# A new written order for a fused attention and expert kernel, with 46 operations on other engines

## The chip, the core and the metric

The kernel runs on one core of a Trainium2 chip. The core has five engines that work side by side, each through its own list of instructions and strictly in that list's order: PE (TensorE, matrix products; its weight loads are shown as PEld), DVE (VectorE), ACT (ScalarE), POOL (GpSimd) and SP (SyncE, which here issues the DMAs). Operands lie in SBUF, products in PSUM. The metric is the device time of one execution in microseconds; less is better.

## What is computed

```python
# q, k, v: 8 batches x 8 heads x 576 tokens x 64; w_gate, w_val: 512 x 1536; w_out: 1536 x 512
k_p = k.reshape(B, H, 72, 8, D).mean(axis=3)
v_p = v.reshape(B, H, 72, 8, D).mean(axis=3)
scores = np.matmul(q, k_p.transpose(0, 1, 3, 2)) / 8
scores = scores - scores.max(axis=-1, keepdims=True)
attn = np.exp(scores)
attn = attn / (attn.sum(axis=-1, keepdims=True) + 1e-09)
x = heads_side_by_side(np.matmul(attn, v_p))     # 4608 tokens x 512
g = x @ w_gate
out = (g / (1 + np.exp(-g)) * (x @ w_val)) @ w_out
```

## The kernel before

**Stages.** The 4608 tokens go through in 9 tiles of 512. The attention of each batch gives its rows of `x` in pieces of at most 128 tokens, 40 in all; one piece is an "answer" (numbers 0 to 39; tile 3 is made of answers 13 to 17). An answer is: scores on PE (L983), maximum and sums on DVE, exponentials on ACT, the shares split into a high half (a 16-bit copy, ACT) and a low half (what the copy lost, L1053 and L1063 with a small second part, on DVE or POOL), a transposing DMA, and the product with the pooled values on PE. Answers 5 to 39 are divided by the softmax sums behind that product, by one DVE operation (L1092) or by eight on ACT, one a head (L1100), and are turned by another DMA into `x` of the expert. Answers 0 to 4 are divided ahead of it (L1034), and their result goes straight into the first tile's `x`: a high half on ACT (L1103) and a low half on DVE (L1107). That tile's products of gate and value read both halves (L1192, L1193, L1194).

**Decoding the weights.** Gate and value weights come as 64-bit numbers in 12 chunks of 128 columns. For each chunk `w_shift` (L732, DVE) moves the low word into place, `w_sign` makes a sign (POOL, DVE or ACT by chunk), `w_abs` (L751, ACT) makes the magnitude of the high word times 2^-112 as a 32-bit float, and `w_join` (L755, DVE) shifts that by three bits and puts the low word's bits in. `w_sums` (L766, ACT) and a PE product (L701) find a scale, and each of a chunk's two halves is then split into 16 bits (`w_high`, L784, ACT or POOL) and the rest (`w_low`, L789, DVE). Chunk by chunk the steps of the first tiles begin as their halves come ready.

**Steps.** Tiles 0 and 1 use `plain_step`. Tiles 2 to 8 use `fast_step`: seven products of six matmuls (L1295) in place of eight, which need sums of the weights (`fast_weights`, once) and of each tile's `x` (`fast_x`). `fast_x` runs twice a tile: one sum on DVE, four differences (L1260), a 16-bit copy on ACT (L1261), two differences for what the copy lost (L1264); L1260 and L1264 go to POOL for the tiles in `SUMS_ON_POOL`, otherwise to DVE. Inside a step the second and third product are joined by a DVE addition (L1360), the seventh and fourth by an ACT copy and a DVE addition (L1365), and the first product waits for an ACT copy (L1355). Behind each step ACT and DVE make the activation (L1139, L1142, L1147). Beside tile 8 the weights of the last product are summed (L1878 ACT, L1884 DVE and others), and then the output stages follow, from about 640 us on.

**The order.** The program is written as many small jobs (an answer, a chunk, a step, ...), and three long tables say whose turn it is at each operation (`NAMES`, `TURNS`) and which job gets which buffer (`HOLDERS`). Each engine's list is thus fixed ahead of time. Tuples of numbers beside them say which engine does certain operations: `DIVIDED_ON_ACT` (answers with L1100), `ON_POOL` (answers among 0 to 4 whose division, L1034, is POOL's), `LOW_ON_DVE` (answers whose low half is DVE's, else POOL's), `XT_ON_DVE` (the low half of the turned result, DVE or POOL), `WEIGHTS_ON_DVE` and `CUT_W_ON_DVE` (parts of `fast_weights` and of the last product's weights), `SUMS_ON_POOL` (tiles whose `fast_x` is POOL's).

Of the kernel before, what the change touches and what calls it, by code (L numbers as in the profile page):

```python
# [2352 lines left out]
```

## Time and profile before

| | |
|---|---|
| time, median of 3 runs | 900.15 us (899.26 to 900.62) |
| profiled execution | 900.0 us, span 898.2 us |
| busy: PE, DVE, ACT, POOL | 876.0, 732.5, 613.5, 193.7 us |
| PE idle, by the waits that the profile names | about 16 us |
| first product of the first tile's steps | 43.0 us |

The profiled execution gives busy time by engine and by stretch, the waits of each engine with what ended them, and every instruction in order of time. A stretch in which PE is busy all the time is bound by PE, and another engine's work there costs nothing until PE has to wait for it.

### The profile page before, as it was taken

Reading aid. Unit: us, or ns where it says so; the run is one execution under the profiler, and the core shown is the slowest. Engines: PE = TensorE matmul, PEld = TensorE weight load, DVE = VectorE, ACT = ScalarE, POOL = GpSimd, SP = SyncE. Lnnn points to the kernel's source line nnn. Section 1 sums busy time; section 2 is a strip of 40 time slices with the busy share of each in tenths; the row PEclk is TensorE's granted clock in tenths of the full one; section 3 lists DMA queues with packets and bytes.
Section 4 is the critical chain, followed back from the end, with each engine's and each line's share of the span. In section 5 each row is a group of like instructions: output and inputs, shape, how many; then the busy total and the mean of one; then the engine's idle time right before and its main releaser. Section 6 shows DMA issues by size and latency. Waiting matters only on the chain. (4 is left out here: it accounts for less than half of the span.)

```text
span 898.2 us, 18137 instructions
## 1 busy us (share of the span) xinstructions
PE 876.0 (98%) x6872; PEld 637.5 (71%) x6872; DVE 732.5 (82%) x1175; ACT 613.5 (68%) x1458; POOL 193.7 (22%) x245
## 2 busy tenths in 40 slices
PE   8899999999999999999999999999999999999998
PEld 5475455447888888888888888888885555555554
DVE  6998998899898788788888777577889686785963
ACT  5999845657768665865666765446558678696783
POOL 2565216558811421110101000023100000000000
PEclk9699999999999999999999999999999999999999
DMA  8968786547467596485475542436264530806212
GB/s 322 325 198 230 204 235 188 116 133 206 112 200 177 118 232 167 140 212 160 133 190 139 145 142 79 154 107 221 95 217 162 186 119 9 343 13 269 83 47 82
DMA packets 139127, 148.39 MB, mean 165 GB/s; under 512 B 85792, under 2 KB 107040, under 8 KB 136736
## 3 DMA queue, kind: packets, MB, share of 16 engines
q1 hardware_dynamic: 139040, 147.24, 54.7%
q8 instruction: 54, 0.88, 0.4%
q14 instruction: 33, 0.27, 0.1%
HBM read 87.29 MB, written 40.89 MB: 143 GB/s over the span
## 5 line engine op out<-in xcount | busy, mean ns | idle before, releaser
L1295 PEld LDWEIGHTS <-mixed 128*128 128x128 f16 x1494 | 144.5, 98 | 20.3 <-issue 2.4
L2148 PE MATMUL ps<-low,wsh 128*128 128x512 bf16 (+1 forms) x420 | 146.7, 358 | 0.0
L1295 PEld LDWEIGHTS <-wgv_h 128*128 128x128 f16 x1328 | 127.8, 98 | 21.0 <-issue 4.4
L1295 PE MATMUL ps<-xc,mixed 128*128 128x256 f16 x996 | 130.7, 273 | 0.6 <-ACT ps L1357 0.6
L1295 PE MATMUL ps<-xc,wgv_h 128*128 128x256 f16 x664 | 116.6, 273 | 1.6 <-DVE ps L1365 1.0
L1295 PE MATMUL ps<-x,wgv_h 128*128 128x256 f16 x664 | 116.7, 273 | 1.3 <-ACT rs L1355 1.3
L1139 ACT ACTIVATE hf<-ps,un 128x512 f32<-128x512 f32 (+1 forms) x111 | 75.5, 681 | 30.3 <-PE ps L1295 17.7
L1295 PE MATMUL ps<-x,wgv_l 128*128 128x256 f16 x332 | 90.5, 273 | 0.0
L1295 PE MATMUL ps<-xc,wgv_l 128*128 128x256 f16 x332 | 90.5, 272 | 0.0
L1147 DVE SCALAR_TENSOR_TENSOR hf<-ps,un,hf 128x512 f32<-128x512 f32 (+1 forms) x111 | 80.7, 729 | 10.7 <-PE ps L1295 8.1
L1193 PE MATMUL ps<-x,wgv_h 128*128 128x512 f16 (+1 forms) x224 | 80.5, 359 | 2.0 <-DVE x L1107 2.0
L1192 PE MATMUL ps<-x,wgv_h 128*128 128x512 f16 (+1 forms) x224 | 80.6, 360 | 0.9 <-ACT x L1103 0.8
L1194 PE MATMUL ps<-x,wgv_l 128*128 128x512 f16 (+1 forms) x224 | 80.5, 359 | 0.0
L1142 DVE SCALAR_TENSOR_TENSOR hf<-hf,ps 128x512 f32<-128x512 f32 (+1 forms) x111 | 73.3, 662 | 8.2 <-ACT hf L1139 8.1
L2148 PEld LDWEIGHTS <-wsh 128*128 128x128 bf16 x420 | 41.0, 98 | 45.2 <-issue 7.6
L2149 PE MATMUL ps<-top,wsl 128*128 128x512 bf16 x192 | 72.8, 379 | 0.0
L1295 PEld LDWEIGHTS <-wgv_l 128*128 128x128 f16 x664 | 64.9, 98 | 7.6
L1295 PE MATMUL ps<-x,mixed 128*128 128x256 f16 x498 | 68.0, 273 | 1.1 <-DVE ps L1360 1.1
L1002 ACT ACTIVATE sc<-ps,mx 128x72 f32<-128x72 f32 (+1 forms) x208 | 63.9, 331 | 0.7
L1357 ACT COPY ps<-ps 128x256 f32<-128x256 f32 x83 | 30.5, 368 | 46.8 <-PE ps L1295 46.3
L1365 DVE TENSOR_TENSOR ps<-ps,rs 128x256 f32<-128x256 f32 x83 | 35.3, 427 | 32.9 <-ACT ps L1364 32.7
L1355 ACT COPY rs<-ps 128x256 f32<-128x256 f32 x83 | 31.0, 373 | 33.2 <-PE ps L1295 22.8
(215 smaller groups left out, 1940.6 us busy)
## 6 DMA issues: line engine op xcount, KB each, us to landing
hd<-hf SPq DMA_DIRECT2D x105, 256.0 KB, 2.7
in<-kv_parts SPq DMA_DIRECT2D x42, 576.0 KB, 5.7
ws<-w_all SPq DMA_DIRECT2D x36, 512.0 KB, 5.4
wgv_h<-hd SPq DMA_DIRECT2D x9, 1536.0 KB, 7.7
wgv_l<-hd SPq DMA_DIRECT2D x9, 1536.0 KB, 7.6
out_t<-ob SPq DMA_DIRECT2D x36, 256.0 KB, 2.3
qt<-q_rows SPq DMA_DIRECT2D x32, 256.0 KB, 4.0
wd<-wf SPq DMA_DIRECT2D x12, 256.0 KB, 2.3
```

The costliest lines, as they stand in the source:

```text
L1002: nc.scalar.activation(sc[:n, h], pss[g][:n, j * SP : (j + 1) * SP], AF.Exp, bias=mx[:n, g, j : j + 1], scale=EXPSCALE, accum_out=sm[:n, h ...
L1139: nc.scalar.activation(hf, gate, AF.Tanh, scale=un[:, c, 0:1])
L1142: nc.vector.scalar_tensor_tensor(out=hf, in0=hf, scalar=1.0, in1=gate, op0=ALU.add, op1=ALU.mult)
L1147: nc.vector.scalar_tensor_tensor(out=out, in0=val, scalar=un[:, c, 2:3], in1=hf, op0=ALU.mult, op1=ALU.mult)
L1192: nc.tensor.matmul(o, wh, x["h"][:, j, a:e], start=(j == 0), stop=False)
L1193: nc.tensor.matmul(o, wh, x["l"][:, j, a:e], start=False, stop=False)
L1194: nc.tensor.matmul(o, wl, x["h"][:, j, a:e], start=False, stop=(j == NJ - 1))
L1295: nc.tensor.matmul(o, a, b, start=begin and j + n == 0, stop=j == HJ - 1 and n == 2, skip_group_check=True,)
L1355: tr = yield op("ACT", 380, lambda: nc.scalar.copy(rs, r), t5, tr)
L1365: tp = yield op("DVE", 430, lambda: nc.vector.tensor_add(s, s, rs), tp)
L2148: nc.tensor.matmul(o, top, where[1][:, c], start=False, stop=False, skip_group_check=True)
L2149: nc.tensor.matmul(o, lo, x_up, start=False, stop=c == HC - 1, skip_group_check=True)
```

## The change

Operations get other engines. `w_abs` of chunks 0, 1, 6 and 11 goes from ACT to DVE, as a product by 2^-112 that leaves the sign in place (the shift by three in `w_join` moves it out). One half's `w_high` goes from ACT to DVE, and the two that were POOL's go to ACT. Nothing is in the new tuples `SOFT_ON_DVE` and `X_ON_DVE`, so those two new paths don't run. The other tuples change as shown. The three tables are written anew throughout; a line or two stand for them.

```diff
-HIGH_ON_POOL = (11, 21)
+HIGH_ON_POOL = ()
+HIGH_ON_DVE = (1,)
+ABS_ON_DVE = (0, 1, 6, 11)
+SOFT_ON_DVE = ()
+X_ON_DVE = ()
...
-DIVIDED_ON_ACT = (14, 16, 18, 21, 22, 38)
+DIVIDED_ON_ACT = (6, 7, 8, 16, 19, 25, 30)
...
-ON_POOL = (1, 2, 3, 4, 5, 6, 7, 8, 9)
-LOW_ON_DVE = (1, 7, 9, 14, 15, 16, 19, 21, 23, 24, 26, 28, 29, 32, 34, 35, 37, 38, 39)
-XT_ON_DVE = (1, 2, 6, 7, 11, 12, 13, 16, 20, 21, 22, 27, 29, 30, 32, 33, 38, 39)
-WEIGHTS_ON_DVE = (1, 2, 4, 11)
-CUT_W_ON_DVE = (3, 4, 7)
-SUMS_ON_POOL = (4,)
+ON_POOL = (0, 1, 2, 3, 4, 5, 6, 7, 8, 9)
+LOW_ON_DVE = (0, 23, 33)
+XT_ON_DVE = (1, 2, 5, 11, 12, 13, 20, 21, 27, 28, 31, 34, 36, 37)
+WEIGHTS_ON_DVE = (1, 2, 4, 6, 9)
+CUT_W_ON_DVE = (2, 3, 4, 7)
+SUMS_ON_POOL = (3, 4, 5, 6, 7, 8)
...
 NAMES = (
-    "keys.0.0 keys.0.1 ask.0 values_load.0.0 warm chunk.0 values_load.0.1 chunk.1 first_fields answer.0 values_in.0.0 ask.1 values_load.0.2 "
+    "warm keys.0.0 keys.0.1 ask.0 values_load.0.1 chunk.0 values_load.0.0 first_fields answer.0 ask.1 values_in.0.1 chunk.1 chunk.2 "
...
     def w_abs(c):
+        if c in ABS_ON_DVE:
+            nc.vector.tensor_single_scalar(chunks[c]["wf"], chunks[c]["high"].bitcast(F32), 2.0**-112, ALU.mult)
+            return
         nc.scalar.activation(chunks[c]["wf"], chunks[c]["high"].bitcast(F32), AF.Abs, scale=2.0**-112)
...
         sw = chunks[c]["sw"]
+        if eng is nc.vector:
+            eng.tensor_scalar(hi, part(c, i), sw[:, i : i + 1], None, op0=ALU.mult)
+            return
...
+        elif 2 * c + i in HIGH_ON_DVE:
+            t = yield op("DVE+", 410, lambda: w_high(c, i, nc.vector), t)
```

The order on the engines is shown at two places. `mixed<-ws` is a chunk's magnitude, `wgv_h` and `wgv_l` the halves of its weights, `x` the first tile's input, `sc` scores, `half` the split shares; line numbers of the kernel after are larger by up to 23.

First ACT at the start of the program, behind the maximum of answer 0's scores. Before:

```order
L751 ACTIVATE mixed<-ws 128x1024
L1002 ACTIVATE sc,sm<-ps,mx 128x72 x8
L766 ACTIVATE wgv_h,wm<-mixed,least 128x512 x2
L1029 ACTIVATE sm<-sm,tiny 128x8
L746 ACTIVATE ws<-ws 128x1024
L751 ACTIVATE mixed<-ws 128x1024
L1017 ACTIVATE sc<-sc 128x576
L784 ACTIVATE wgv_h<-mixed,sw 128x512 x2
L1029 ACTIVATE sm<-sm,tiny 128x8
L1047 CAST half_142<-sc 128x512
L1049 CAST half_142<-sc 128x2x32 x2
```

After:

```order
L1012 ACTIVATE sc,sm<-ps,mx 128x72 x8
L1039 ACTIVATE sm<-sm,tiny 128x8
L773 ACTIVATE wgv_h,wm<-mixed,least 128x512 x2
L1062 CAST half_142<-sc 128x512
L1064 CAST half_142<-sc 128x2x32 x2
L1027 ACTIVATE sc<-sc 128x576
L750 ACTIVATE ws<-ws 128x1024
L1039 ACTIVATE sm<-sm,tiny 128x8
L794 ACTIVATE wgv_h<-mixed,sw 128x512
L750 ACTIVATE ws<-ws 128x1024
L758 ACTIVATE mixed<-ws 128x1024
```

Two magnitudes that stood here on ACT are gone from it (of chunks 0 and 1), the exponentials of answer 0 come right behind the score's maximum, and a chunk's first high half is alone here.

DVE ahead of the low half of the first piece's second `x` (L1107, after L1125). Before:

```order
L1020 TENSOR_REDUCE sm<-sc 128x8
L1107 SCALAR_TENSOR_TENSOR x<-ps,rr,x 128x4x128
L732 TENSOR_SCALAR ws<-ws 128x1024
L706 TENSOR_SCALAR p2w<-ps 128x2
L709 RECIPROCAL sw<-p2w 128x2
L1625 TENSOR_REDUCE spare<-in 128x144
L1024 RECIPROCAL ri<-sm 128x8
L789 SCALAR_TENSOR_TENSOR wgv_l<-mixed,sw,wgv_h 128x512 x2
L1107 SCALAR_TENSOR_TENSOR x<-ps,rr,x 128x4x128
```

After:

```order
L1030 TENSOR_REDUCE sm<-sc 128x8
L710 TENSOR_SCALAR p2w<-ps 128x2
L713 RECIPROCAL sw<-p2w 128x2
L1646 TENSOR_REDUCE spare<-in 128x144
L1034 RECIPROCAL ri<-sm 128x8
L736 TENSOR_SCALAR ws<-ws 128x1024
L710 TENSOR_SCALAR p2w<-ps 128x2
L713 RECIPROCAL sw<-p2w 128x2
L1125 SCALAR_TENSOR_TENSOR x<-ps,rr,x 128x4x128
L799 SCALAR_TENSOR_TENSOR wgv_l<-mixed,sw,wgv_h 128x512
L762 SCALAR_TENSOR_TENSOR mixed<-mixed,ws 128x1024
L799 SCALAR_TENSOR_TENSOR wgv_l<-mixed,sw,wgv_h 128x512
```

Before, two low halves of weights (L789) stand directly ahead of that `x`; after, `x` (the L1125 row) stands ahead of the two (L799), with a chunk's `w_join` (L762) between them.

Second, the sums of tile 3's `x`. Before, they stand in DVE's list, among the additions of tile 2's steps:

```order
L1260 TENSOR_TENSOR fx<-fx 128x256
L1142 SCALAR_TENSOR_TENSOR hf<-hf,ps 128x512
L1360 TENSOR_TENSOR ps<-ps,rs 128x256
L1625 TENSOR_REDUCE box<-in 128x144 x2
L1142 SCALAR_TENSOR_TENSOR hf<-hf,ps 128x512
L1147 SCALAR_TENSOR_TENSOR hf<-ps,un,hf 128x512
L1360 TENSOR_TENSOR ps<-ps,rs 128x256
L1264 TENSOR_TENSOR xc<-fx,xc 128x512
L1024 RECIPROCAL ri<-sm 128x8
L1365 TENSOR_TENSOR ps<-ps,rs 128x256
L1264 TENSOR_TENSOR xc<-fx,xc 128x512
```

After, they stand in POOL's list, among low halves of answers (L1078, L1079) and parts of `fast_weights` (L1240):

```order
L1282 TENSOR_TENSOR xc<-fx,xc 128x512
L1254 TENSOR_TENSOR wgv_l<-room,wgv_h 128x256
L1078 TENSOR_TENSOR half_142<-sc,half_142 128x8x56
L1079 TENSOR_TENSOR half_142<-sc,half_142 128x128
L1282 TENSOR_TENSOR xc<-fx,xc 128x512
L1078 TENSOR_TENSOR half_143<-sc,half_143 128x8x56
L1079 TENSOR_TENSOR half_143<-sc,half_143 128x128
L1278 TENSOR_TENSOR fx<-fx 128x256 x4
L1240 TENSOR_TENSOR fw<-fw 128x256
L1282 TENSOR_TENSOR xc<-fx,xc 128x512 x2
L1840 TENSOR_TENSOR box<-sc,box 128x512
```

The four differences (L1260, now L1278) and the two of the second half (L1264, now L1282) have moved from DVE to POOL, and the operations of other jobs that they stand behind have changed with them.

## Rows read from the trace of the kernel before

**Rows 1.** The page: busy us, share of the span and instructions of each engine.

```profile
PE 876.0 (98%) x6872; PEld 637.5 (71%) x6872; DVE 732.5 (82%) x1175; ACT 613.5 (68%) x1458; POOL 193.7 (22%) x245
```

**Rows 2.** Windows by stage: length, busy us (instructions) by engine, PE clock, DMA share, GB/s.

```profile
25.00:50.00 25.00, 21.32 (x132) 12.51 (x131) 24.65 (x42) 23.44 (x64) 14.44 (x16) 0.66 0.98 308
...
75.00:100.00 25.00, 23.24 (x150) 11.73 (x149) 22.99 (x39) 23.31 (x66) 13.46 (x19) 1.00 0.89 244
...
200.00:250.00 50.00, 48.02 (x469) 38.12 (x468) 44.79 (x79) 35.50 (x114) 40.99 (x48) 1.00 0.66 173
...
300.00:400.00 100.00, 100.00 (x1046) 87.32 (x1044) 84.49 (x167) 65.56 (x187) 19.10 (x21) 1.00 0.73 187
...
600.00:650.00 50.00, 48.27 (x433) 42.73 (x433) 40.70 (x68) 28.41 (x61) 11.35 (x8) 1.00 0.45 156
```

**Rows 3.** What PE waited for: its line, releaser, us in total, times, longest.

```profile
PE ps L1193 <- DVE x L1107: 2.0, 1, 2.0
...
PE ps L701 <- ACT wgv_h L766: 1.7, 2, 1.3
PE ps L1082 <- DMA pt<-half: 1.6, 3, 0.7
PE ps L1295 <- ACT rs L1355: 1.3, 3, 0.6
PE ps L1295 <- DVE ps L1360: 1.1, 3, 0.4
PE ps L1295 <- DVE ps L1365: 1.0, 2, 0.5
```

**Rows 4.** VectorE ahead of the first step: start us, us, line, operation [idle before <-releaser].

```profile
18.39 0.46 DVE L1010 TENSOR_REDUCE mx<-ps 128x4 f32<-128x288 f32 x1 [1.34 <-PE ps L983]
...
42.29 2.25 DVE L789 SCALAR_TENSOR_TENSOR wgv_l<-mixed,sw,wgv_h 128x512 f16<-128x512 f32 x2
44.46 0.74 DVE L1107 SCALAR_TENSOR_TENSOR x<-ps,rr,x 128x512 f16<-128x512 f32 x1
```

**Rows 5.** Groups by line and form: xcount | busy us, mean ns of one | idle before.

```profile
L1260 DVE TENSOR_TENSOR fx<-fx 128x256 f32<-128x256 f32 x48 | 22.8, 474 | 0.6
...
L1063 POOL TENSOR_TENSOR half<-sc,half 128x448 f16<-128x448 f32 x15 | 16.8, 1118 | 65.3 <-ACT half L1058 54.0 <-issue 11.3
L1264 DVE TENSOR_TENSOR xc<-fx,xc 128x512 f16<-128x512 f32 x24 | 16.6, 699 | 0.9 <-ACT xc L1261 0.9
...
L1092 DVE TENSOR_TENSOR sc<-ps,ri 128x512 f32<-128x512 f32 x23 | 15.4, 681 | 1.7 <-PE ps L1088 1.3
...
L784 ACT ACTIVATE wgv_h<-mixed,sw 128x512 f16<-128x512 f32 x22 | 15.2, 719 | 0.8 <-DVE ri L1024 0.7
...
L751 ACT ACTIVATE mixed<-ws 128x1024 f32<-128x1024 f32 x12 | 14.1, 1173 | 1.5 <-DMA ws<-w_all 1.5
...
L1884 DVE TENSOR_TENSOR wf<-wf 128x512 f32<-128x512 f32 x12 | 12.9, 1077 | 0.2
...
L732 DVE TENSOR_SCALAR ws<-ws 128x1024 uint32<-128x1024 uint32 x12 | 9.0, 747 | 4.1 <-DMA ws<-w_all 4.1
...
L1100 ACT ACTIVATE sc<-ps,ri 128x64 f32<-128x64 f32 x40 | 8.8, 334 | 2.0 <-DVE fw L1216 1.2 <-PE ps L1088 0.8
L1063 DVE TENSOR_TENSOR half<-sc,half 128x448 f16<-128x448 f32 x13 | 8.5, 653 | 0.7 <-ACT half L1058 0.6
...
L1260 POOL TENSOR_TENSOR fx<-fx 128x256 f32<-128x256 f32 x8 | 6.2, 770 | 9.5 <-DVE fx L1256 9.1
...
L1264 POOL TENSOR_TENSOR xc<-fx,xc 128x512 f16<-128x512 f32 x4 | 4.6, 1157 | 3.5 <-ACT xc L1261 3.5
...
L2023 DVE TENSOR_TENSOR wgv_h<-wgv_h 128x512 f32<-128x512 f32 x6 | 4.0, 683 | 0.0
```

**Rows 6.** VectorE at the end of tile 3's sums; columns as in rows 4.

```profile
267.35 0.68 DVE L1264 TENSOR_TENSOR xc<-fx,xc 128x512 f16<-128x512 f32 x1
```

**Rows 7.** PE at the first products that read them; columns as in rows 4.

```profile
269.06 0.38 PE L1295 MATMUL ps<-xc,wgv_h 128*128 128x256 f16 x2
```

More of the change, by code (lines that the diff above doesn't have):

```diff
@@ L87 @@
 NAMES = (
[64 rows of a table removed]
[63 rows of a table added]
+    "stored.3.0.1.1 returned operand_room "
 )
 TURNS = (
[102 rows of a table removed]
[102 rows of a table added]
 )
 HOLDERS = {
+    "val": (
[9 rows of a table added]
+    ),
     "ws": (
-        "0/raw 5/raw 7/wo2 13/wo1 19/raw 21/raw 33/wo2 34/wo1 49/raw 62/wo2 72/wo1 82/wo2 97/wo1 "
+        "1/raw 5/raw 11/wo2 12/wo1 20/raw 29/raw 37/wo2 47/wo1 50/raw 69/wo2 77/wo1 85/wo2 96/wo1 "
     ),
     "qt": (
-        "2/1 11/1 16/1 20/0 32/0 50/1 69/1 78/1 79/0 90/1 121/0 130/1 143/0 144/1 153/0 157/1 174/0 178/1 192/0 209/1 213/0 230/1 231/0 243/0 244/1 "
-        "260/1 262/0 267/1 278/0 282/1 287/0 307/1 313/0 321/1 331/0 353/1 359/0 362/1 367/0 378/1 471/0 483/1 483/0 512/1 512/0 540/1 540/0 567/1 "
-        "567/0 "
-    ),
-    "val": (
[9 rows of a table removed]
+        "3/1 9/1 15/1 19/0 33/0 40/1 52/0 67/1 76/1 99/1 105/0 126/1 135/0 146/1 150/0 155/1 164/0 178/1 193/0 208/0 211/1 226/1 228/0 244/1 245/0 "
+        "258/1 259/0 274/0 275/1 291/1 292/0 308/1 320/0 321/1 343/0 353/1 358/0 366/1 368/0 375/1 471/0 485/1 485/0 512/1 512/0 540/1 540/0 568/1 "
+        "568/0 "
     ),
     "sc": (
-        "9/0 15/1 27/0 30/1 40/0 66/1 73/0 88/1 106/0 116/1 133/0 139/1 150/0 154/1 161/0 177/1 185/0 200/1 204/0 217/1 221/0 235/1 241/0 251/1 258/0 "
-        "264/1 273/0 281/1 286/0 306/1 311/0 320/1 328/0 350/1 354/0 360/1 364/0 370/1 380/0 385/1 "
+        "8/0 14/1 26/0 30/1 38/0 62/1 74/0 93/1 103/0 114/1 134/0 136/1 148/0 154/1 162/0 177/1 187/0 199/1 205/0 217/1 220/0 237/1 243/0 249/1 256/0 "
+        "263/1 270/0 281/1 286/0 307/1 312/0 319/1 326/0 348/1 356/0 361/1 365/0 371/1 379/0 386/1 "
     ),
     "att": (
[9 rows of a table removed]
[9 rows of a table added]
     ),
@@ L295 @@
     "mid": (
[3 rows of a table removed]
[3 rows of a table added]
     ),
     "half": (
-        "9/0 15/1 27/0 30/1 40/0 66/1 73/0 88/1 106/0 116/1 133/0 139/1 150/0 154/1 161/0 177/1 185/0 200/1 204/0 221/1 217/0 235/1 241/0 251/1 258/0 "
-        "264/1 273/0 281/1 286/0 306/1 311/0 320/1 328/0 350/1 354/0 360/1 364/0 370/1 380/0 385/1 "
+        "8/0 14/1 26/0 30/1 38/0 62/1 74/0 93/1 103/0 114/1 134/0 136/1 148/0 154/1 162/0 177/1 187/0 199/1 205/0 217/0 220/1 237/1 243/0 249/1 256/0 "
+        "263/1 270/0 281/1 286/0 307/1 312/0 319/1 326/0 348/1 356/0 361/1 365/0 371/1 379/0 386/1 "
@@ L303 @@
     ),
     "pt": (
-        "15/1 9/0 27/1 30/0 40/1 66/0 73/1 88/0 106/1 116/0 133/1 139/0 150/1 154/0 161/1 177/0 185/1 200/0 204/1 221/0 217/1 235/0 241/1 251/0 258/1 "
-        "264/0 273/1 281/0 286/1 306/0 311/1 320/0 328/1 350/0 354/1 360/0 364/1 370/0 380/1 385/0 "
+        "8/0 14/1 26/1 30/0 38/1 62/0 74/1 93/0 103/1 114/0 134/1 136/0 148/1 154/0 162/1 177/0 187/1 199/0 205/1 217/1 220/0 237/0 243/1 249/0 256/1 "
+        "263/0 270/1 281/0 286/1 307/0 312/1 319/0 326/1 348/0 356/1 361/0 365/1 371/0 379/1 386/0 "
@@ L307 @@
     ),
     "x": (
-        "35/x1 65/wo0 134/x0 173/x1 206/wo0 250/x0 302/x1 346/wo0 371/x0 425/x1 425/wo0 593/x0 "
+        "31/x1 57/wo0 131/x0 172/x1 207/wo0 248/x0 299/x1 341/wo0 369/x0 425/x1 425/wo0 593/x0 "
     ),
     "wv": (
-        "15/acc1 9/acc1 27/acc1 30/acc1 40/acc1 66/acc1 73/acc1 88/acc1 106/acc1 116/acc1 133/acc1 133/acc1 "
+        "14/acc1 8/acc1 26/acc1 30/acc1 38/acc1 62/acc1 74/acc1 93/acc1 103/acc1 114/acc1 134/acc1 134/acc1 "
     ),
     "gate": (
[9 rows of a table removed]
[9 rows of a table added]
     ),
     "hf": (
[9 rows of a table removed]
[9 rows of a table added]
@@ L335 @@
     ),
     "load": (
-        "85/0 92/0 94/0 108/0 115/0 120/0 123/0 128/0 129/0 136/0 137/0 142/0 181/0 182/0 183/0 188/0 193/0 194/0 223/0 224/0 225/0 233/0 236/0 239/0 "
-        "268/0 269/0 271/0 277/0 279/0 290/0 291/0 291/0 291/0 315/0 316/0 322/0 327/0 330/0 334/0 291/0 291/0 291/0 291/0 291/0 291/0 291/0 291/0 "
-        "291/0 "
+        "86/0 87/0 108/0 112/0 117/0 118/0 125/0 129/0 130/0 133/0 140/0 141/0 179/0 181/0 182/0 191/0 192/0 194/0 224/0 225/0 227/0 232/0 233/0 "
+        "235/0 267/0 268/0 272/0 276/0 279/0 280/0 290/0 290/0 313/0 317/0 290/0 322/0 327/0 329/0 334/0 290/0 290/0 290/0 290/0 290/0 290/0 290/0 "
@@ L340 @@
+        "290/0 290/0 "
     ),
     "xt1": (
-        "66/2 73/2 88/2 106/2 116/2 "
+        "62/2 74/2 93/2 103/2 114/2 "
     ),
     "fw": (
-        "141/f_more 145/f_room 155/f_more 156/f_room 170/f_room 175/f_more 184/f_room 187/f_more 195/f_room 198/f_more 203/f_room 214/f_more "
+        "139/f_more 144/f_room 156/f_more 157/f_room 168/f_room 173/f_more 183/f_room 185/f_more 195/f_room 198/f_more 203/f_room 214/f_more "
         "425/f_room "
@@ L348 @@
     "xt": (
-        "133/0 139/1 150/0 154/1 161/0 177/1 185/0 200/1 204/0 217/0 221/1 235/0 241/1 251/0 258/1 264/0 273/1 281/0 286/1 306/0 311/1 320/0 328/1 "
-        "350/0 354/1 360/0 364/1 370/0 380/1 385/0 "
+        "134/0 136/1 148/0 162/0 154/1 177/1 187/0 199/1 205/0 220/1 217/0 237/0 243/1 249/0 256/1 263/0 270/1 281/0 286/1 307/0 312/1 319/0 326/1 "
+        "348/0 356/1 361/0 365/1 371/0 386/0 379/1 "
     ),
     "xc": (
-        "163/wo1 215/early 253/wo1 293/early 329/wo1 373/early 400/wo1 425/early "
+        "166/wo1 218/early 252/wo1 295/early 330/wo1 374/early 407/wo1 425/early "
     ),
     "f": (
-        "163/f_own 163/f_own 215/f_own 215/f_own 253/f_own 253/f_own 293/f_own 293/f_own 329/f_own 329/f_own 373/f_own 373/f_own 400/f_own 400/f_own "
+        "166/f_own 166/f_own 218/f_own 218/f_own 252/f_own 252/f_own 295/f_own 295/f_own 330/f_own 330/f_own 374/f_own 374/f_own 407/f_own 407/f_own "
         "425/f_own "
@@ L359 @@
     "rs": (
[4 rows of a table removed]
[4 rows of a table added]
     ),
     "wf": (
-        "291/left 291/left 291/left 291/left 291/left 291/left 291/left 291/left 291/left 291/left 291/left 291/left "
+        "290/left 290/left 290/left 290/left 290/left 290/left 290/left 290/left 290/left 290/left 290/left 290/left "
     ),
     "set": (
-        "479/0 479/1 479/0 479/1 479/0 479/1 479/0 510/1 510/0 510/1 510/0 510/1 510/0 510/1 538/0 538/1 538/0 538/1 538/0 538/1 538/0 563/1 563/0 "
-        "563/1 563/0 563/1 563/0 563/1 "
+        "480/0 480/1 480/0 480/1 480/0 480/1 480/0 507/1 507/0 507/1 507/0 507/1 507/0 507/1 536/0 536/1 536/0 536/1 536/0 536/1 536/0 562/1 562/0 "
+        "562/1 562/0 562/1 562/0 562/1 "
     ),
@@ L1042, in parts, with soft_high @@
         return main, left, over
-    def soft_high(n, sc, half):
+    def soft_high(eng, n, sc, half):
         main, left, over = parts(n, sc, half)
+        if eng is not nc.scalar:
+            eng.tensor_copy(out=main[:, 0], in_=sc[:n, :, :KMAIN])
+            for d in range(2):
+                eng.tensor_copy(out=left[:, d], in_=over)
+            return
         nc.scalar.copy(main[:, 0], sc[:n, :, :KMAIN])
@@ L1100, in divided_by_head, with x_high @@
             nc.scalar.activation(out[:, cs], ps[:, cs], AF.Copy, scale=ri[:n, h : h + 1])
-    def x_high(psv, n, x, off, ratio):
+    def x_high(eng, psv, n, x, off, ratio):
+        if eng is nc.vector:
+            eng.tensor_scalar(x["h"][:, :, off : off + n], psv, ratio[:, 0:1], None, op0=ALU.mult)
+            return
         nc.scalar.activation(x["h"][:, :, off : off + n], psv, AF.Copy, scale=ratio[:, 0:1])
@@ L1410, in chunk @@
         tf = yield flag(("decoded", c - 3, 2)) if c > 2 else flag("start")
-        ta = yield op("ACT", 1139, lambda: w_abs(c), t, tf)
+        eng, ns = ("DVE+", 680) if c in ABS_ON_DVE else ("ACT", 1139)
+        ta = yield op(eng, ns, lambda: w_abs(c), t, tf)
         t = yield op("DVE+", 1220, lambda: w_join(c), ts, ta)
@@ L1763, in answer @@
             half = halves[h]
-            tp = yield op("ACT", 910, lambda: soft_high(m, sc, half), tp, th)
+            eng, ns, on = ("DVE+", 760, nc.vector) if t["n"] in SOFT_ON_DVE else ("ACT", 910, nc.scalar)
+            tp = yield op(eng, ns, lambda: soft_high(on, m, sc, half), tp, th)
             tp = yield low_part(t["n"], soft_low, m, sc, half, tp)
@@ L1793, in answer @@
             put("pt", u, tp)
-            tp = yield op("ACT", 684, lambda: x_high(ps["o"], m, x, off, r), tp, tr)
+            eng, ns, on = ("DVE", 640, nc.vector) if t["n"] in X_ON_DVE else ("ACT", 684, nc.scalar)
+            tp = yield op(eng, ns, lambda: x_high(on, ps["o"], m, x, off, r), tp, tr)
             tp = yield op("DVE", 750, lambda: x_low(ps["o"], m, x, off, r), tp)
```

415 rows, old and new, of tables (HOLDERS, NAMES, TURNS) are left out of this document.

## The prediction

> **What bounds the kernel now.** I read the page's shares first, then the busy time by stage, then what PE waited for, and at the places found so the rows in order of time. PE is busy 876.0 of 898.2 us [rows 1], so all that an order of the same matmuls can win is the idle rest of some 22 us, part of it ahead of the first operand and behind the last product. By stages the rest lies in three places [rows 2]. In 25 to 50 us DVE is busy 24.65 of 25 us and ACT 23.44, and in 75 to 100 us still 22.99 and 23.31, while PE has gaps: the decoding of the weights sets the pace there. In 200 to 250 us PE lacks 1.98 us and POOL is busy 40.99 of 50. In 600 to 650 us, beside the last tile, PE lacks 1.73. Between, in 300 to 400 us for one, PE is busy all 100 us: there a lighter DVE is worth nothing. The waits name the same places [rows 3]: one of 2.0 us at the first step, for the low half of `x` on DVE; 1.7 for the sums of two weight chunks on ACT; 1.6 for three transposing DMAs; and 1.3, 1.1 and 1.0 for the copies and additions inside the fast steps.
>
> **The start.** Directly ahead of that awaited `x` (44.46 us) DVE makes two low halves of weights for 2.25 us, from 42.29 [rows 4]. The new order puts them behind it. In exchange two magnitudes stand ahead of it on DVE. A DVE magnitude is not in the trace; the nearest row is the shift, one input and as many elements, 0.747 us [rows 5], and I take that; as an upper end the ACT form's 1.173 holds. One high half of 512 elements is also new on DVE: between half a shift, 0.37, and the 0.68 of a two-input operation of that size (L1092), say 0.5. The division of answer 0 leaves DVE for POOL; L1092's 0.68 stands for it. In sum 2 x 0.747 + 0.5 - 2.25 - 0.68 = -0.9 us on DVE. ACT loses three magnitudes and three high halves from this stretch, 3 x 1.173 + 3 x 0.719 = 5.7 us, so ACT, which made the other half of `x` only shortly before, no longer ties the start. DVE also sat idle 1.34 us at 18.39 us for PE's scores [rows 4]; whether that goes with the exponentials' earlier place I can't see. The first step should thus start 0.9 to 2.2 us sooner, up to 2.7 if the two magnitudes fill idle time.
>
> **What the decode leaves of it.** An earlier first step is kept only if the later chunks come earlier as well. I counted the operations in each list up to the last half of chunk 11. On DVE four magnitudes and a high half are added, 4 x 0.747 + 0.5 = 3.5 us; three divisions L1092 go (answers 6, 7 and 8 to ACT), 3 x 0.681 = 2.0; one low half goes (0.65, [rows 5]), one pooling of values (twice an L1092, 1.36), and one each of three operations of L1092's size (2.0). That is -2.6 us on the engine that was busy almost throughout. On ACT sixteen head divisions are added, 16 x 0.334 = 5.3, and one high half, 0.72; four magnitudes go, 4.7, and one activation, about 0.7: +0.6 us. PE's largest wait in this stretch was for ACT (1.7 us for the sums, [rows 3]), and ACT was busy over nine tenths of it. So of 0.9 to 2.7 us an upper end of 2.6 can be kept if DVE decides, and the lower end is a loss of 0.6 if ACT does. In the middle of the decode DVE's list up to chunks 5 to 8 is longer than before, since magnitudes come ahead of what was put off; only from chunk 9 on is it shorter. I take -1.0 us, a little over a third of DVE's gain, as both engines are needed for each chunk.
>
> **From 115 to 300 us.** Here PE waits about 3.5 us: transposing DMAs behind POOL's and DVE's low halves, one division L1092, some chains of steps. The new order may spare up to 2.5 of it. But it gives POOL, the fullest here, the sums of tile 3: eight differences of 0.770 in place of 0.474 and four of 1.157 in place of 0.699 [rows 5], that is 10.8 us of POOL for 6.6 of DVE, and most low halves as well, 1.118 instead of 0.653 each. The margin at tile 3 is thin: on DVE the last difference ends at 267.35 + 0.68 = 268.03 [rows 6], and the first products that read it begin at 269.06 [rows 7], 1.03 us later. On POOL the part behind the 16-bit copy takes 2 x 1.157 = 2.3 us in place of 2 x 0.699 = 1.4, and the part ahead 4 x 0.770 = 3.1 in place of 1.9; a low half (1.118 and its small second part) or a weight difference in front delays it by 1 to 2 us more. If the first sum starts when it did, 0.9 + 1.2 = 2.1 us are added to the chain, against a margin of 1.03: about +1 us, nothing if POOL gets to it sooner, +3 with a low half in front. The two effects nearly cancel; I take -0.5, with -2.5 and +3 as ends.
>
> **Steps of tiles 3 to 8.** Moving the sums of five more tiles takes 5 x 6.6 = 33 us off DVE and puts 54 on POOL. In full stretches that buys nothing. Where PE does wait inside steps, 1.3 + 1.1 + 1.0 us in all [rows 3], it is for chains of one ACT copy or DVE addition, and the third product then stood behind its second with little between. In the old order ten steps have one product or none between the second and third product; in the new two have. Against that, two more steps have only one product between the fifth and first. With DVE freer, most of the 1.1 and 1.0 should go, less of the 1.3: I take -1.0, with -2.5 and +1 as ends. In the output stages, matmuls and operations stay as they were and PE is full: 0.
>
> **Sum.** 900.0 - 1.0 - 0.5 - 1.0 = 897.5 us, made against the profiled execution; it stands 0.15 below the median, well inside the runs' own spread, and I don't correct for it.
>
> **A shared port.** The twelve additions L1884 on DVE take 1.077 us beside POOL's work, where the same form in L2023, without POOL, takes 0.683 [rows 5]: 4.7 us in all, beside 11.35 us of POOL in that window [rows 2]. L1264 with a mean of 0.699 hardly lengthens. The Trainium skill ("SBUF — State Buffer", section "Who interferes with whom") calls the port pair of VectorE and GpSimd an exclusive lock, on which a two-input SBUF operation of VectorE is fully blocked while GpSimd reads; that speaks against giving GpSimd so much. The L1884 row agrees with it. By that row's 4.7 / 11.35 = 0.4 us lost per us of POOL, POOL's 54 us more would cost DVE 22 us; spread over stages where DVE lost 33 us of its own, it leaves DVE lighter. It matters only where a two-input operation lies ahead of an addition that PE awaits.
>
> **Rivals.** First, *the whole start is kept*: the decode follows DVE's -2.6, and the step chains and the middle give 1.5 each: 900.0 - 2.6 - 3.0 = 894.4. For it speaks that DVE was the fuller engine at 25 to 50 us; against it that ACT's work grows. Second, *nothing comes of it*: the change does what it says on DVE and ACT, but PE's decode wait moves from the first step to a later chunk (ACT +0.6), tile 3 costs +1, and the steps give -1.0: 900.6, no change. For it: ACT's and DVE's near-equal load in 75 to 100 us. Third, *POOL late, with the lock*: at tiles 3 and 4, where POOL carries low halves, sums and weight parts in one list, its sums and the low halves behind them come late, +3 at tile 3 and +1 at each of two transposes, while the start keeps its lower end, +0.6, and the steps, with DVE operations of 0.7 us stretched to 1.1 ahead of their additions, win nothing: 900.0 + 5 - 0.5 = 904.5. It decides once POOL's list reaches tile 3's last difference more than 1.03 us later than DVE's did. POOL's 41 of 50 us ahead of that stage speak for it; that its 250 to 300 us were light before, against it.
>
> **How the numbers follow.** The forecast, 895.5 to 899.5, gets 0.45; the first rival 0.13, the second 0.24, the third 0.18. A measurement here can tell about 0.2%, 1.8 us, so faster is below 898.35 and slower above 901.95. Of the forecast's 0.45 some 0.37 lies below 898.35; with the first rival that makes 0.50 faster; the second rival and the forecast's upper part make 0.32; the third is 0.18. The range leaves out the far end of the first rival and most of the third: 893.0 to 902.5.
>
> **What would show it.** Right: the first L1193 product (there at another line number) starts before 44.3 us; the last decode waits of PE sum to no more than 1.7 us; PE's waits for L1360's additions fall under 0.5 us; DVE's busy time falls by 25 to 40 us, POOL's rises by 55 to 85. Wrong: a PE wait for a POOL difference at tile 3 or 4, a later end of the decode than before although the start is earlier, or a magnitude on DVE well over 0.75 us.

## The result

The kernel after takes 890.93 us (median of 4 runs, 889.84 to 892.01), against 900.38 before: a ratio of 0.9895, 95% interval 0.9877 to 0.9913. It is faster by 9.5 us. The forecast was 897.5 with a range of 893.0 to 902.5: right in its sign and well short in its size, so that the time lies below the range.

The profiled execution took 892.0 us, 8.0 less than the profiled one of before (spans 890.1 and 898.2). Its page, where the line answers to [rows 1]:

```profile
PE 871.2 (98%) x6853; PEld 639.6 (72%) x6872; DVE 696.2 (78%) x1088; ACT 612.4 (69%) x1463; POOL 269.4 (30%) x334
```

DVE lost 36 us of work and POOL gained 76, as the tuples say. PE's busy time fell by 4.8 us (this trace lacks 19 matmul records; the second profile of the same kernel, which lacks none, has 866.9 us, 9.1 less). That is not less work. A matmul of the fast steps counts as busy for 0.27 us, but the next one can start 0.11 us after it, so some 0.16 us of each gap is counted as busy; and in 25 to 50 us PE's granted clock was 0.85 instead of 0.66. What PE waited for in the kernel after (line, releaser, us in total, times, longest), beside [rows 3]:

```profile
PE ps L1210 <- DVE hf L1165: 2.7, 1, 2.7
PE ps L1097 <- DMA pt<-half: 2.2, 1, 2.2
...
PE ps L916 <- DMA vr<-v_left: 2.1, 1, 2.1
...
PE ps L1210 <- DVE hf L1160: 1.2, 1, 1.2
...
PE ps L1313 <- DVE ps L1378: 0.3, 1, 0.3
```

All but the last of these lie ahead of 115 us. Of the waits inside steps in [rows 3] (L1295 there, L1313 here) 0.3 us is left, of 3.4 and more. By stages, with the columns of [rows 2]; first four stretches of the kernel before, which stand nowhere above, then the same of the kernel after:

```profile
0.00:115.00 115.00, 103.55 (x736) 64.13 (x737) 103.58 (x187) 96.79 (x276) 52.55 (x85) 0.93 0.84 255
115.00:300.00 185.00, 181.51 (x1528) 124.10 (x1526) 164.55 (x277) 124.71 (x420) 92.29 (x112) 1.00 0.62 164
300.00:560.00 260.00, 259.51 (x2645) 227.89 (x2643) 215.00 (x421) 168.24 (x455) 31.77 (x36) 1.00 0.59 158
560.00:650.00 90.00, 87.50 (x790) 77.42 (x788) 65.96 (x110) 47.96 (x103) 17.12 (x12) 1.00 0.42 141
```

```profile
0.00:115.00 115.00, 101.37 (x716) 64.64 (x717) 100.35 (x179) 95.13 (x287) 54.99 (x82) 0.93 0.85 255
115.00:300.00 185.00, 184.91 (x1586) 127.78 (x1585) 161.02 (x272) 123.64 (x408) 113.17 (x139) 1.00 0.66 169
300.00:560.00 260.00, 260.00 (x2647) 229.25 (x2645) 188.81 (x349) 169.60 (x462) 83.37 (x99) 1.00 0.62 159
560.00:650.00 90.00, 89.73 (x818) 80.47 (x816) 68.78 (x119) 52.85 (x110) 17.90 (x15) 1.00 0.41 138
```

From 115 to 650 us PE was idle 3.49 + 0.49 + 2.50 = 6.5 us before and 0.36 us after. In the first 115 us it is idle more than before, 13.6 instead of 11.5 us. So in this profile the gain lies wholly behind the decoding of the weights, where the prediction had put 1.5 us of it.

Equal stretches of time hold different work once one kernel is ahead, so a second measure helps. I counted the matmuls of each kernel by their weight loads, each at the median spacing that its form has in the trace of before, and noted when each amount of work was reached. The table gives how much later (+) or earlier (-) a kernel got there than the kernel before, at the work that before had done by 77, 179, 284, 467 and 630 us, and at the end of the span. All kernels are those of the next section; "after again" is the unedited kernel in a later run.

| us, against before | 77 | 179 | 284 | 467 | 630 | end |
|---|---|---|---|---|---|---|
| after | -0.1 | +1.7 | -2.9 | -4.3 | -6.3 | -8.1 |
| after again | -1.6 | -1.4 | -6.0 | -7.4 | -9.5 | -11.2 |
| order only | +0.8 | +2.4 | +4.6 | +10.3 | +10.5 | +8.9 |
| choices only | +2.2 | +8.8 | +10.0 | +12.2 | +13.4 | +12.9 |
| old order, sums | +0.1 | +0.2 | +0.9 | +1.1 | +1.7 | +1.3 |
| new order, sums | +0.7 | +2.3 | +0.7 | +5.0 | +4.3 | +2.7 |
| sums back on DVE | -1.4 | -1.4 | -2.3 | -1.5 | -2.1 | -3.8 |
| tile 3's sums back | 0.0 | -1.4 | -2.3 | -3.7 | -5.8 | -7.5 |
| four small tuples back | -0.9 | -1.9 | -4.6 | -2.4 | -4.1 | -5.7 |
| low halves back | -0.8 | -3.0 | -5.3 | -4.8 | -6.7 | -8.4 |
| magnitudes back | -1.2 | +0.2 | -3.7 | -5.1 | -7.2 | -8.9 |
| answer 7's low half on DVE | -0.2 | -2.4 | -6.6 | -8.0 | -10.1 | -11.8 |
| and L1165 moved | -0.1 | -2.2 | -6.8 | -8.2 | -10.3 | -12.0 |

"After" and "after again" are one program. They differ by 3.1 us at 179 us and by nothing behind it: from there each gains 9.8 us on the kernel before (of the 11.2 us of "after again" 1.4 lie ahead of that). The start varies by that much from one execution to the next, and the granted clock varies with it (0.93 against 1.00 in 50 to 75 us, 0.89 against 1.00 in 100 to 115 us), so single profiles can't rank changes of a microsecond there.

### The profile page after: what moved, and what is told of

The parts are those of the page before. It is cut to its first block, busy times and chain, and to the rows that moved or that the text cites. A ratio compares the mean times of both kernels' runs of the same rounds, so it can differ in the third digit from the quotient of the medians.

```text
span 890.1 us, 18154 instructions
## 1 busy us (share of the span) xinstructions
PE 871.2 (98%) x6853; PEld 639.6 (72%) x6872; DVE 696.2 (78%) x1088; ACT 612.4 (69%) x1463; POOL 269.4 (30%) x334
## 4 chain that ended last, share of the span: by engine, by line
PE 87%; DVE 4%; DMA 3%; issue 2%; ACT 2%; POOL 2%; SPq 0%; DVEq 0%; POOLq 0%; ACTq 0%
PE ps L1313 41%; PE ps L2156 10%; PE ps L2172 9%; PE ps L2171 9%; PE ps L993 3%; PE ps L1210 3%; PE ps L1211 3%; PE ps L1212 3%; DMA ws<-w_all 2%; PE ps L1103 1%; PE ps L1102 1%; PE ps L1097 1%; PE ps L1609 1%; DVE wgv_l L799 1%; DVE hf L1165 1%
## 5 line engine op out<-in xcount | busy, mean ns | idle before, releaser
L1313 PEld LDWEIGHTS <-mixed 128*128 128x128 f16 x1494 | 144.7, 98 | 17.6 <-issue 0.4
L2171 PE MATMUL ps<-low,wsh 128*128 128x512 bf16 (+1 forms) x408 | 142.1, 357 | 0.4
L1313 PEld LDWEIGHTS <-wgv_h 128*128 128x128 f16 x1328 | 127.7, 98 | 16.8 <-issue 0.2
L1313 PE MATMUL ps<-xc,mixed 128*128 128x256 f16 x996 | 130.7, 273 | 0.0
L1313 PE MATMUL ps<-x,wgv_h 128*128 128x256 f16 x664 | 116.8, 273 | 0.0
L1313 PE MATMUL ps<-xc,wgv_h 128*128 128x256 f16 x664 | 116.6, 273 | 0.1
L1165 DVE SCALAR_TENSOR_TENSOR hf<-ps,un,hf 128x512 f32<-128x512 f32 (+1 forms) x111 | 80.6, 729 | 13.2 <-PE ps L1313 9.0
L1313 PE MATMUL ps<-xc,wgv_l 128*128 128x256 f16 x332 | 90.5, 273 | 0.0
L1313 PE MATMUL ps<-x,wgv_l 128*128 128x256 f16 x332 | 90.5, 273 | 0.0
L1211 PE MATMUL ps<-x,wgv_h 128*128 128x512 f16 (+1 forms) x224 | 80.6, 360 | 0.1
L1313 PEld LDWEIGHTS <-wgv_l 128*128 128x128 f16 x664 | 65.0, 98 | 7.5
L1313 PE MATMUL ps<-x,mixed 128*128 128x256 f16 x498 | 67.9, 273 | 0.3 <-DVE ps L1378 0.3
L1078 POOL TENSOR_TENSOR half<-sc,half 128x448 f16<-128x448 f32 (+1 forms) x33 | 41.3, 1251 | 81.4 <-ACT half L1073 69.6
L1375 ACT COPY ps<-ps 128x256 f32<-128x256 f32 x83 | 30.3, 365 | 46.5 <-PE ps L1313 46.3
```

The lines of the kernel that those rows point to most:

```text
L1078: eng.tensor_sub(a[:, :, SP:], sc[:n, :, : P - SP], a[:, :, : P - SP])
L1165: nc.vector.scalar_tensor_tensor(out=out, in0=val, scalar=un[:, c, 2:3], in1=hf, op0=ALU.mult, op1=ALU.mult)
L1211: nc.tensor.matmul(o, wh, x["l"][:, j, a:e], start=False, stop=False)
L1313: nc.tensor.matmul(o, a, b, start=begin and j + n == 0, stop=j == HJ - 1 and n == 2, skip_group_check=True,)
L2171: nc.tensor.matmul(o, top, where[1][:, c], start=False, stop=False, skip_group_check=True)
```

## Experiments

**Order or choices.** Two theories: the written order removes the stalls (A), or the lighter DVE does (B). The first run has the new order and the old choices:

```diff
-HIGH_ON_DVE = (1,)
-ABS_ON_DVE = (0, 1, 6, 11)
-DIVIDED_ON_ACT = (6, 7, 8, 16, 19, 25, 30)
-LOW_ON_DVE = (0, 23, 33)
-SUMS_ON_POOL = (3, 4, 5, 6, 7, 8)
+HIGH_ON_DVE = ()
+ABS_ON_DVE = ()
+DIVIDED_ON_ACT = (14, 16, 18, 21, 22, 38)
+LOW_ON_DVE = (1, 7, 9, 14, 15, 16, 19, 21, 23, 24, 26, 28, 29, 32, 34, 35, 37, 38, 39)
+SUMS_ON_POOL = (4,)
...
```

The remaining tuples, `HIGH_ON_POOL`, `ON_POOL`, `XT_ON_DVE`, `WEIGHTS_ON_DVE` and `CUT_W_ON_DVE` are as before too.

> The new written order with every choice of an engine put back to the kernel before (eight tuples as before, the two new ones empty). Theory A, the order itself removes the stalls: the waits inside the fast steps stay small (under 1 us in all after 115 us) and the time is 889 to 894. Theory B, the stalls go because DVE is lighter after 250 us: the waits on L1378 and L1383 and the stalls beside tile 8 come back, 4 us or more of the 8 lost, time 896 to 902.

It took 908.3 us (906.8 to 911.3), ratio 1.0098 (1.007 to 1.0125): slower than either kernel. The second run has the old order and the new choices (`NAMES`, `TURNS` and `HOLDERS` of before in the kernel after).

> The old written order (the three tables of the kernel before) with the new choices of an engine. Theory A, the order: the waits of the kernel before remain or grow, since POOL's longer sums stand where DVE's stood; time 899 to 910. Theory B, the lighter DVE: most of the step waits go, 890 to 896.

It took 913.1 us, ratio 1.0149 (1.0129 to 1.0169). Both theories fall in the form I gave them. One half of the change costs 8 us, the other 13, and together they save 9.5. Why, the waits tell. With the new order alone, PE's waits after 115 us:

```profile
PE ps L1313 <- DVE hf L1165: 4.4, 7, 1.2
PE ps L1313 <- DVE p2s L710: 1.9, 1, 1.9
PE ps L993 <- DVE sc L1107: 1.5, 1, 1.5
PE ps L1313 <- ACT ps L1375: 1.3, 2, 1.0
PE ps L1313 <- DVE ps L1383: 1.2, 3, 0.8
```

All but one are waits for DVE: L1165 (the activation that frees a bank for the next step) and L1107 (a division) stand in a list that now also holds the operations which this order was written for on POOL and ACT. With the choices alone, in 80 to 300 us:

```profile
PE ps L1097 <- DMA pt<-half: 5.2, 4, 3.3
PE ps L993 <- DVE sc L1107: 1.7, 1, 1.7
PE ps L705 <- ACT wgv_h L773: 1.3, 1, 1.3
```

Here the low halves are POOL's, of which the old order had nearly half on DVE, and PE waits 5.2 us for the transposing DMAs that follow them. In 100 to 115 us, where the longest of these waits lies, PE's granted clock was 0.84, and 6.6 of the 12.9 us are lost between 77 and 179 us. One stretch does belong to the order alone: beside tile 8. Windows of the new order with the old choices, 300 to 560 us and then 575 to 665 us, which hold tile 8 (this kernel is there some 12 us later):

```profile
300.00:560.00 260.00, 255.47 (x2603) 223.04 (x2602) 206.56 (x405) 167.75 (x466) 35.64 (x41) 1.00 0.59 153
575.00:665.00 90.00, 89.39 (x812) 79.98 (x811) 69.80 (x121) 52.23 (x109) 15.97 (x12) 1.00 0.41 140
```

PE is idle 4.5 us in the first, but in the second 0.6 against 2.5 before, although DVE and ACT have the old choices there. The count by weight loads says the same of all runs: over the work that the kernel before did from 580 to 650 us, each of the eleven profiles with the new order gains 3.0 to 3.3 us, and the two others with the old order gain nothing (0.0 and 0.8 lost).

**The sums of x.** The largest choice alone, taken back in the kernel after (`SUMS_ON_POOL = (4,)`):

> The kernel after with the sums of x for tiles 3 and 5 to 8 back on DVE (33 us of DVE, 54 us of POOL back); all else, the order too, as after. Theory A, the order: within 1.5 us of the kernel after, 889 to 892.5. Theory B, the lighter DVE: the stalls inside fast steps return, 2 to 5 us, 893 to 897.

896.9 us (10 runs, 896.2 to 901.2), ratio 0.9966 (0.9949 to 0.9983): of the gain after 179 us 7.4 of 9.8 us are lost, in stretches beside tiles 2 to 7, as B had it. But a lighter DVE by itself is not the reason, as the same tuple in the old order shows (kernel before with `SUMS_ON_POOL = (3, 4, 5, 6, 7, 8)`):

> The kernel before, its written order too, with one tuple of the change alone: the sums of x for tiles 3 and 5 to 8 on POOL as well. Theory A, order and choice belong together: POOL's longer sums stand at places made for DVE's, PE waits at tile 3 or later for a POOL difference or a copy behind one, and the time is 899 to 906. Theory B, a lighter DVE is enough: the step waits (3.4 us in the kernel before) halve, no wait on POOL, 895 to 898.

901.2 us, ratio 1.0008 (0.9991 to 1.0025): no change, with 24 us less on DVE. Its waits beside tile 8 and PE's idle time there:

```profile
PE ps L1295 <- DVE ps L1360: 0.6, 2, 0.4
PE ps L1295 <- ACT rs L1355: 0.6, 1, 0.6
PE ps L1295 <- ACT ps L1357: 0.6, 1, 0.6
PE ps L1295 <- DVE ps L1365: 0.5, 1, 0.5
```

```profile
560.00:650.00 90.00, 87.56 (x790) 77.41 (x789) 66.63 (x111) 47.73 (x102) 17.11 (x12) 1.00 0.40 136
```

2.44 us of idle PE as in the kernel before; but here DVE has as much to do as before (66.63 and 65.96 us). Where it has 20 us less, from 300 to 560 us, PE is idle longer, 1.41 instead of 0.49 us:

```profile
300.00:560.00 260.00, 258.59 (x2634) 226.75 (x2632) 194.66 (x373) 167.99 (x454) 73.21 (x84) 1.00 0.62 157
```

A's time came true, its mechanism did not: there is no wait for POOL. What these waits hang on, by the rows, is not DVE's load but what stands directly ahead of the awaited addition in DVE's list; no run moved such a row by itself. Two rows of DVE and then PE's row at the longest wait for L1360 in the kernel before (start us, us):

```profile
593.97 1.29 DVE L1884 TENSOR_TENSOR wf<-wf 128x512 f32<-128x512 f32 x1
595.18 0.42 DVE L1360 TENSOR_TENSOR ps<-ps,rs 128x256 f32<-128x256 f32 x1
```

```profile
595.65 0.81 PE L1295 MATMUL ps<-x,mixed 128*128 128x256 f16 x6 [0.41 <-DVE ps L1360]
```

By the profile the second product had ended at 593.64 us, two other products stand between it and the third, and still the addition came too late: it stood behind an L1884, which took 1.29 us beside POOL's L1880 (at 593.44 and 594.66 us) instead of 0.69 (at 592.37). The old order with the sums on POOL has the same two rows, L1884 with 1.24 us, and so the same wait. In the new order the twelve additions take 0.74 us on the mean, with the old choices 0.85, against 1.08 before. The reverse, the new order with only the sums on POOL and the other tuples old:

> The new order with every choice as before except the sums of x, which go to POOL as in the change. It took 908.3 with none of the new choices and 889 to 892 with all. Theory A, the sums are the choice that the order most needs after 200 us: 7 us or more come back, 896 to 901. Theory B, the many small choices (low halves, divisions, weight parts) carry as much: 902 to 907.

902.8 us (901.0 to 904.7), ratio 1.0022 (1.0012 to 1.0032): 5.5 of the 18.6 us between "order only" and the kernel after come back. That lies in B's range: counted this way, the small choices carry more than the sums. Taken back from the whole change, though, the sums weigh most (7.2 us between the medians, against 4.5 for the four small tuples below): what a choice is worth depends on which others are in place. Tile 3's sums alone back on DVE (`SUMS_ON_POOL = (4, 5, 6, 7, 8)`):

> The kernel after with tile 3's sums alone back on DVE. With all five tiles' back it lost 7 us, of which about 3.5 between 220 and 260 us of matmul work, where tile 3's sums stand. If each tile's sums delay the steps beside them: 892 to 894.5. If it is DVE's load over the whole stretch: under 891.

892.8 us (892.5 to 895.5), ratio 0.9915 (0.9896 to 0.9934), by the ratios 2 to 3 us over the kernel after (0.9884 and 0.9895). The first reading holds: between 179 and 284 us this kernel gains 0.9 us where the kernel after gains 4.6, and nothing differs later. PE's waits name the place:

```profile
PE ps L1313 <- DVE ps L1383: 1.7, 2, 1.4
...
PE ps L993 <- DVE sc L1107: 0.9, 1, 0.9
```

**The small choices.** Divisions, turned low halves and weight parts as before, the rest as after:

```diff
-DIVIDED_ON_ACT = (6, 7, 8, 16, 19, 25, 30)
-XT_ON_DVE = (1, 2, 5, 11, 12, 13, 20, 21, 27, 28, 31, 34, 36, 37)
-WEIGHTS_ON_DVE = (1, 2, 4, 6, 9)
-CUT_W_ON_DVE = (2, 3, 4, 7)
+DIVIDED_ON_ACT = (14, 16, 18, 21, 22, 38)
+XT_ON_DVE = (1, 2, 6, 7, 11, 12, 13, 16, 20, 21, 22, 27, 29, 30, 32, 33, 38, 39)
+WEIGHTS_ON_DVE = (1, 2, 4, 11)
+CUT_W_ON_DVE = (3, 4, 7)
```

> The kernel after with four small tuples as before (divisions on ACT, low half of the turned result, parts of fast_weights and of the last product's weights); sums, low halves, magnitudes and order as after. If these carry a share of what the order needs: 893 to 898, with waits in 115 to 250 us and in the decode. If they are nearly free: within 1.5 us of the kernel after, 888.5 to 892.

894.2 us (893.8 to 895.1), ratio 0.9925 (0.991 to 0.994), with DVE's busy time the same as in the kernel after (696.5 and 696.2 us), and ACT's and POOL's a little lower (610.0 and 266.0 us, against 612.4 and 269.4). They cost 3.3 to 4.5 us (against 890.9 and 889.7) without more load on any engine. PE's longest waits after 115 us are 1.6 us for L710, which comes behind a turned low half (L1838) that is back on DVE, and 1.0 us for L1375, behind head divisions (L1115) back on ACT: what counts is that an operation runs where the order expects it. The low halves of all answers as before (`LOW_ON_DVE` of before):

> The kernel after with the low halves of answers on DVE or POOL as in the kernel before (19 answers on DVE instead of 3; among them answer 7, whose second part took 4.25 us on POOL and made PE wait 2.2 us at 107 us). Theory A, the order: the wait at 107 us goes, PE's other waits don't grow, 887 to 891. Theory B, the lighter DVE: the wait at 107 us goes but 12 us more on DVE bring back waits of 2 to 4 us after 115 us, 890 to 895.

890.8 us, ratio 0.9896 (0.9874 to 0.9919), the same as the kernel after within the interval. The wait at 107 us is gone, and what that gave, DVE's added 15 us took back between 179 and 467 us: as B had it in the mechanism; the time lies in the ranges of both.

**The start.** The kernel after again, on the chip of the next three:

> The changed kernel itself, unedited, so that the others of this set have it on the same chip. 889.5 to 892.5; PE waits 2.2 us for the transposing DMA at 107 us and 2.7 us for L1165 at 51.7 us again if these belong to the order, not if they were chance.

889.7 us (888.8 to 890.8), ratio 0.9884 (0.9865 to 0.9903); both waits are there again (2.4 and 2.0 us). Magnitudes and high half back on ACT (`ABS_ON_DVE = ()`, `HIGH_ON_DVE = ()`):

> The kernel after with the four magnitudes and the one high half back on ACT, order unchanged. If these moves make the earlier first step (41.6 instead of 43.0 us): the first L1210 at 43 us or later and the lag before 60 us of matmul work 2 to 5 us larger, 892 to 896. If the written order makes it: within 1 us of the kernel after.

891.3 us (890.8 to 892.8), 1.6 over "after again", between the two expectations. The first product is at 42.14 us instead of 41.59, still ahead of 43.0: the order makes most of the earlier start, the moved magnitudes the smaller part.

In the kernel after, POOL's low half of answer 7 takes far longer than usual, and the products behind it wait; POOL, then PE, in order of time (start us, us, line, operation [idle before <-releaser]):

```profile
98.15 1.55 POOL L1078 TENSOR_TENSOR half<-sc,half 128x448 f16<-128x448 f32 x1 [1.03 <-ACT half L1073]
99.66 4.25 POOL L1079 TENSOR_TENSOR half<-sc,half 128x128 f16<-128x128 f32 x1
...
104.59 1.02 POOL L1078 TENSOR_TENSOR half<-sc,half 64x448 f16<-64x448 f32 x1
```

```profile
107.26 0.51 PE L1097 MATMUL ps<-spare,pt 128*128 128x512 f16 x1 [2.19 <-DMA pt<-half]
```

L1079, usually much shorter (the mean of its 26 by form, this one included, is 0.63 us: xcount | busy us, mean ns of one | idle before), takes 4.25 us:

```profile
L1079 POOL TENSOR_TENSOR half<-sc,half 128x128 f16<-128x128 f32 x26 | 16.5, 634 | 0.0
```

PE waits 2.19 us, and in this execution the clock is lower behind that, at 0.53 on the mean where 0.5 is the lower of its two levels, 1.2 GHz. From PE's idle stretch on (PE clock ahead of the DMA share):

```profile
104.70:107.26 2.56, 0.37 (x2) 0.00 (x1) 0.88 (x1) 1.50 (x4) 1.30 (x2) 1.00 0.93 157
107.26:110.89 3.63, 3.63 (x25) 2.12 (x26) 1.78 (x4) 2.18 (x9) 0.79 (x2) 0.53 1.05 276
110.89:113.00 2.11, 2.11 (x11) 0.88 (x9) 2.11 (x3) 2.11 (x6) 1.25 (x2) 1.00 1.09 341
```

In "after again", with a wait of 2.0 us at that place, the clock stayed at 1.00 from 100 to 115 us. A wait of this length may or may not cost the clock. Nor does the wait always come. "Tile 3's sums back" is the same program up to there; its L1079 got through and the two small operations on POOL behind it were held instead, which take 0.19 and 0.50 us in the kernel after. PE has no wait for the transposing DMA there:

```profile
100.24 0.44 POOL L1079 TENSOR_TENSOR half<-sc,half 128x128 f16<-128x128 f32 x1
100.63 0.73 POOL L1472 TENSOR_TENSOR p2w<-p2w 128x1 f32<-128x1 f32 x1
101.44 3.05 POOL L1478 TENSOR_TENSOR un<-p2w,mt 128x3 f32<-128x3 f32 x3
```

So one choice altered, `LOW_ON_DVE = (0, 7, 23, 33)`:

> The kernel after with one choice altered: the low half of answer 7 on DVE instead of POOL. Theory A (POOL's 4.25 us in the second part of this low half, beside DVE's operations, made the wait of 2.2 us and the slower clock behind it): the wait at 107 us goes, 2 to 4 us less than the kernel after, 887 to 889. Theory B (DVE is full there, and PE waits for the weights instead): a wait for weight halves or sums in its place, within 1 us of the kernel after.

888.0 us (887.8 to 888.2), ratio 0.9864 (0.9847 to 0.9882): 1.7 us under "after again", none of whose four runs is as low. Theory A holds, with a little less than its 2 to 4 us: PE is busy from 85 to 115 us without a gap and at the full clock, with DVE at 29.69 of 30 us:

```profile
85.00:115.00 30.00, 30.00 (x220) 15.75 (x219) 29.69 (x53) 28.87 (x94) 11.94 (x22) 1.00 0.92 246
```

This kernel is faster than both that were given. Last, from it, one turn of the order moved (in words, as DVE's list changes by it):

```diff
 L1160 (activation of the first step)
 L736 (shift of a weight chunk)
+L1165
 L799 x2 (two low halves of weights)
-L1165
```

> As the kernel with answer 7's low half on DVE, and one operation moved in the written order: L1165 of the first step ahead of two low halves of weights (L799), which take 2.29 us in front of it. If PE's wait of 2.7 us at 51.7 us is DVE's order alone: the wait falls below 0.6 us and the time by 1 to 2.5 us more, 885 to 888. If the decode behind binds: the wait goes but the time stays within 0.7 us of the kernel without this move, and the same microseconds come back as waits for weights by 100 us.

889.1 us (888.0 to 890.2), ratio 0.9879 (0.986 to 0.9897): no gain, and 1.2 us more than without the move, where the second reading had allowed 0.7. The wait for L1165, 3.0 us in the kernel that this one starts from, shrank to 0.4, and the time came back in other waits, as that reading had it:

```profile
PE ps L705 <- DVE mxv L873: 1.8, 1, 1.8
...
PE ps L1212 <- DVE wgv_l L799: 1.0, 1, 1.0
PE ps L1210 <- DVE hf L1165: 0.4, 1, 0.4
```

A wait taken away at one place appeared at the next. It would fit that DVE's work as a whole is the bound in this stretch, but that is not shown: ahead of the moved operation DVE sits idle 1.5 us until a chunk's DMA lands, and the two low halves took 3.02 us behind it instead of 2.29 ahead of it.

## Why the prediction was wrong

**The start** was forecast to come 0.9 to 2.2 us sooner; the first L1193 (now L1211) came at 42.01 instead of 45.26 us, 3.2 sooner, more than the 2.7 of the upper end (the step's very first product came 1.4 sooner, at 41.60). The operations' prices held: a magnitude on DVE takes 0.705 us where 0.747 was taken. What the decode leaves was put at -1.0, by DVE's and ACT's lists; it is -1.4 in one profile and +1.7 in the other. By the count of weight loads the two are 5.2 and 5.5 us ahead at the work that before had done by 49 us, and by 58 us that is +0.8 and -0.6. New waits took the place of the old one (2.7 and 1.2 us for the activations of the first steps, 2.2 for a transposing DMA), which the second rival had in kind. So the earlier start was put too small; what is left of it was about right, and is smaller than what the start varies by.

**From 115 to 300 us** -0.5 was taken, with -2.5 as the end. Measured: -4.6 between 179 and 284 us in both profiles, and as much from 115 to 300. This step failed, twice. I let a loss at tile 3 cancel the gain: POOL's longer chain against a margin of 1.03 us [rows 6, 7]. There was no loss. POOL did the second half's differences from 263.98 for 2.27 us, PE waited for none of it, and with the new order the same sums on DVE cost 2 to 3 us more, because there they stand ahead of additions that PE does wait for. With the old order the move gains nothing in this stretch ("old order, sums": 0.7 us lost from 179 to 284), so the sums had not held PE up there; it is the new lists as a whole that do not hold it. And I capped the gain at 2.5 of "about 3.5 us" of named waits: PE's idle time fell from 3.49 to 0.09 us, and seven gaps with 0.16 us more in each make up most of the rest.

**Steps of tiles 3 to 8** were put at -1.0, with -2.5 as the end; the gain from 284 us to the end is 5.2 us in both profiles. The term itself was mis-sized: of the named step waits nearly all went, not a third. A stall also cost more than its wait: PE's spacing shows each gap of the kernel before with some 0.16 us on top (the product at 595.65 us waited 0.41 and started 0.57 late), the part of a gap that counts as busy. And the reason I gave, "with DVE freer", was wrong, as the sums in the old order show. So was "with little between": the counts, ten places before and two after, hold, but only one of the ten has a wait of PE in the kernel before (0.25 us, at 615.94 us). At the two longer waits for L1360 (212.71 and 595.65 us) more than one product stands between. There the addition stood on DVE behind a pooling of values (L1625, 1.34 us) and behind an L1884 beside POOL. The prediction named that case under the shared port, a two-input operation ahead of an addition that PE awaits, and did not look for it in the rows. That the sign came out right owes more to the new order as a whole than to the reasons given.

**The rivals.** The first came nearest in time (894.4), for a wrong reason: not the start, the middle and the steps gave the gain. The third, POOL late under the port, has its one case at 107 us and not at tile 3: 2.2 us and a slower clock; its sum, 904.5, takes 0.5 us off where its words put 0.6 on, which makes 905.6. Of the things that were to show the forecast right, DVE's fall (36 us), POOL's rise (76), the L1360 waits (0.3, under 0.5) and the first step came true; the decode's waits did not.

What none of my cases held is that the order and the choices are one object (the tuples differ in 64 entries, not in the 46 of the title). I costed each move by load and by the waits it touched, against the old order; either half alone makes the kernel slower. Which job gets which buffer (`HOLDERS`) went with the order in every run; no run parts the two.
